# Two attention blocks on one core: full-width matmul passes as two column tiles of 64 in place of four of 32, with constants, one small transfer and the planner's numbers changed

## The chip, the cores and the metric

The kernel runs on one core of a Trainium2 chip. The core has a matrix engine (PE), a vector engine (DVE), a scalar engine (ACT), a general engine (POOL) and a queue engine (SP) that issues transfers; ACT issues some too. Each runs its own stream of instructions in order, and they meet at semaphores. The metric is the device time of one execution in microseconds (us). The median of three runs of the kernel before is 323.95 us (320.75 to 328.06).

## The reference

Two independent blocks, A and B, each on an input of 2,048 rows and 640 columns, with 32 heads of 20 columns. Their outputs stand side by side.

```python
# A: softmax attention
scores = jnp.einsum("bhqd,bhkd->bhqk", q, k) * (Dh ** -0.5)
p = _softmax(scores, axis=-1)
o = jnp.einsum("bhqk,bhkd->bhqd", p, v)
# B: linear attention
phi = lambda t: jnp.where(t > 0, t + 1, jnp.exp(t)) + 1e-6
pq, pk = phi(q), phi(k)
kv = jnp.einsum("bhsd,bhse->bhde", pk, v)
z = jnp.einsum("bhsd->bhd", pk)
num = jnp.einsum("bhqd,bhde->bhqe", pq, kv)
den = jnp.einsum("bhqd,bhd->bhq", pq, z)[..., None] + 1e-6
o = num / den
```

In both, `q`, `k` and `v` are thirds of `x @ wqkv`, and the block ends with `o @ wo`. All inputs are bfloat16.

## The kernel before

**Block A without a score matrix.** The scores are small, so the exponential is taken to second order in them: per head, what a query needs of all keys is a table of sums over products of key columns. For each of 16 row tiles (`t_kv`, L1312) PE makes K and V in two halves of 320 columns; ACT copies and squares; DVE makes the products of key columns (`t_feat`, L1364 and L1369, 1.8 us each, 32 in all); and PE adds the tile into the table (`t_T`, L1390), one 32-column product for each head, 242 columns wide. At the end `t_Tfin` (L1397) turns the table, multiplies it with selection matrices `P` and spreads it with a mask (L1456, into f_Tu). On the query side `t_qj` makes q transposed, SP writes it to DRAM (f_Qd), `t_psi` reads it back shifted into one of three slots (f_big, L1589 and L1590), DVE makes the products of query columns (L1601), and `t_pv` runs twelve passes of 512 columns on f_Tu. `t_norm` sends the sums of the weights through DRAM (f_Rc, f_Nd, f_Rbc) for a reciprocal, and `t_out` multiplies by `wo`. A guard (`t_guard`, and L1625) checks that the scores are in range.

**Block B.** `b_tasks` (L1802) makes K and V, phi of K, and sums `phi(k)` times v over row tiles (`kvmm`, L1839; `kvpost` adds into f_kva). `kvfin` (L1868) masks out what belongs to other heads, and sums phi(k) into f_zn. These 640 numbers are written to DRAM (f_Zd, `z1`, L1891) and read back in another order (`z2`, L1893) to form f_kvZ (`zfin`). The table times `wo` gives f_Md, read back as f_Mp. `qden` then makes phi of q, the denominators (`dmm`, 32 columns wide, L2000), their reciprocals, and `numout` the output.

**Column tiles.** Every matmul pass with up to 128 stationary columns goes through `fm` (L1104). It cuts the stationary operand into pieces of 32 columns, each in its own column strip of the array, and issues a load and a matmul for each. The state products of `t_T`, the small q passes of `t_qs` (L1555), the guard's products, `tmm`, `cmm` and `dmm` place 32-column tiles by themselves and do not go through `fm`. Transposes and the selection products use the full width.

**Order of work.** Nothing of the order is written by hand beyond the loads. Every piece of work is a `_Task` with an engine, an assumed duration, dependencies and a priority. `_Plan.step` (L833) takes the engine and task that can start first by its assumed times, the lower priority number first among those ready together, and emits its instructions. So assumed durations (as in `job`, L1073, where a pass counts columns / 2400 us plus 0.003, or 0.1 if that is more) and the priorities in `_C` (L947) together set the order on every engine. `spd` (L1099) emits transfers to SP or ACT; as the queue is in order, a transfer that waits for a semaphore holds back all behind it.

**Constants.** `consts` makes the identity matrix and clears buffers. `mid_consts` (L1208) makes the rest as one chain of tasks, each after the one before: DVE makes scale vectors (L1225 to L1232), POOL an iota, DVE masks and the memsets of f_kva, f_dn and f_kvN (L1239 to L1249), POOL the selection matrices P (L1257, 17 copies), then five times an iota on POOL into the same buffer and two mask operations on DVE (L1266, L1270, L1271).

Of the kernel before, what the change touches and what calls it, by code (L numbers as in the profile page):

```python
# [6 lines left out]
F32 = mybir.dt.float32  # L7
BF16 = mybir.dt.bfloat16
I32 = mybir.dt.int32
# [921 lines left out]
def _off(d):  # L931

    if d is None:
# [12 lines left out]
_WS = 176  # L946
_C = dict(q=0.62, qs=0.04, ks=0.0, kd=0.02, bk=1.68, bks=0.0, bq=-2.52, bo=0.0, out=2.14, pv=0.0, fe=3.88,  # L947
          psi=5.12, r=-4.73, f=0.5, nm=3.12, op=6.09, kv=1.52, npo=0.16, bqs=0.05, bd=0.02, bn=4.94)


class _Fast:

    AUX = (4, 5, 6, 7)
    GB = 3
    NF = 2
    NK = 3
# [27 lines left out]
    def alloc(self):  # L984
# [36 lines left out]
        self.kvZ = self.sb("f_kvZ", [128, N_DC, 32], BF16)  # L1021
        self.zs = self.sb("f_zs", [128, N_DC, 8], F32)
        self.zn = self.sb("f_zn", [128, 2, N_DC], F32)
        self.M32 = self.sb("f_M32", [128, 32], BF16)
# [25 lines left out]
        self.zt = self.sb("f_zt", [128, 128], BF16)  # L1050
        self.it = rb0[:, 0:360].bitcast(I32).rearrange("p (k n) -> p k n", k=2)
        self.rp = self.sb("f_rp", [128, 4], F32)
# [51 lines left out]
    def fm(self, out, lhsT, rhs, start, stop, reads, writes, inc=True, sgc=False):  # L1104
        m = lhsT.shape[1]
        for j in range(0, m, 32):
            k = min(j + 32, m)
            self.sch.mm(out[j:k], lhsT[:, j:k], rhs, start=start, stop=stop, reads=reads, writes=writes, tp=(0, j),
                        inc=inc and k == m, sgc=sgc)
# [3 lines left out]
    def loads(self):  # L1113
# [44 lines left out]
        def perm(x, c):  # L1158
# [4 lines left out]
        self.ew[0] = plan.add(_Task("none", 0.0, lambda t: None), [plan.add(_Task(  # L1163
            "act", 0.9, lambda x, c=c: perm(x, c), prio=1.0), (e0,)) for c in range(N_DC)])
        self.exB[1] = xpose(self.xB, b2, 1, "xB")
# [5 lines left out]
        def permB(x, c):  # L1171
            self.copy(x.eng, self.wB[:, 0, c, :].rearrange("p (a h) -> p a h", h=N_HEADS),
                      self.w0B[:, c, :].rearrange("p (h a) -> p a h", a=D_HEAD), ("w0B",), (("wB", 0, c),))
        self.ewB[0] = plan.add(_Task("none", 0.0, lambda t: None), [plan.add(_Task(
            "act", 0.75, lambda x, c=c: permB(x, c), prio=2.2), (e1,)) for c in range(N_DC)])
        self.ewoB = plain(self.woB[:], self.Bwo.rearrange("(c p) n -> p c n", p=128), "woB", 0.8)
# [13 lines left out]
    def consts(self):  # L1190
        sch, ps, it = self.sch, self.ps, self.it
        sch.op("dve", lambda e: e.memset(self.zt[:], 0.0), writes=("zt",))
        sch.op("pool", lambda e: e.iota(it[:, 0, 0:128], [[1, 128]], base=0, channel_multiplier=-1), writes=("it0",))
        sch.op("dve", lambda e: e.memset(self.warm[:], 0.0), writes=("warm",))
        sch.op("act", lambda e: e.activation(self.warm[:], self.warm[:], AF.Exp), writes=("warm",))
        sch.op("dve", lambda e: e.tensor_scalar(self.ident[:], it[:, 0, 0:128], 0.0, None, op0=ALU.is_equal),
               reads=("it0",), writes=("ident",))
# [10 lines left out]
    def mid_consts(self):  # L1208
        sch, it, rp, plan = self.sch, self.it, self.rp, self.plan
        scr = self.pqT[:, 0, :].bitcast(F32)  # L1210
        last = self.event(1.5)
        cl = (1.0 + _RNG * _RNG / 8.0) * float(D_HEAD) ** -0.5
        q = 0.5 / D_HEAD

        def task(eng, dur, *ops):
            nonlocal last

            def fn(t):
                for f, r, w in ops:
                    sch.op(eng, f, reads=r, writes=w)  # L1220
            last = plan.add(_Task(eng, dur, fn, prio=2.4), (last,))
        K = ("pqT", 0, 0)

        task("dve", 1.6,
             (lambda e: e.tensor_scalar(rp[:, 0:1], it[:, 0, 0:1], -1.0, None, op0=ALU.mult), ("it0",), ("rp",)),  # L1225
             *[(lambda e, c=c, at=at, v=v: e.tensor_scalar(rp[:, c:c + 1], rp[:, 0:1], at, v, op0=ALU.is_ge, op1=ALU.mult),
# [7 lines left out]

        task("pool", 0.5,
             (lambda e: e.iota(it[:, 1, 0:120], [[1, 6], [6, 20]], base=0, channel_multiplier=-1), (), ("it1",)))
        mf, e6, m32 = scr[0:120, 0:120], scr[0:120, 120:126], scr[:, 128:160]
        task("dve", 1.5,
             (lambda e: e.tensor_scalar(mf, it[0:120, 1, 0:120], 0.0, None, op0=ALU.is_equal), ("it1",), (K,)),  # L1239
             (lambda e: e.tensor_reduce(e6, mf.rearrange("p (h a) -> p h a", a=20), axis=AX.X, op=ALU.add), (K,), (K,)),  # L1240
             (lambda e: e.memset(self.M6[:], 1.0), (), ("M6",)),
             (lambda e: e.tensor_copy(self.M6[0:120, :], e6), (K,), ("M6",)),
             (lambda e: e.memset(self.M1[:], 1.0), (), ("M1",)),
             (lambda e: e.tensor_reduce(m32, self.ident[:].rearrange("p (a h) -> p h a", h=N_HEADS), axis=AX.X,
                                        op=ALU.add), ("ident",), (K,)),
             (lambda e: e.tensor_copy(self.M32[:], m32), (K,), ("M32",)),
             (lambda e: e.memset(self.kvacc[:], 0.0), (), ("kva0",)),
             (lambda e: e.memset(self.mask, 0.0), (), ("mask0",)),
             (lambda e: e.memset(self.kvN[:], 0.0), (), ("kvN0",)))  # L1249
        ops = [(lambda e: e.memset(self.GW[:], 0.0), (), ("GW",)),  # L1250
               (lambda e: e.tensor_copy(self.GW[:, 8:14], self.M6[0:120, :]), ("M6",), ("GW",))]

        for x, (d, r) in enumerate(_SL):
            o = _off(d)[1]
            for a, n, b in ((0, 20 - r, o + r), (20 - r, r, o)):
                if n:
                    ops.append((lambda e, x=x, a=a, n=n, b=b: e.tensor_copy(  # L1257
                        self.P[:, x, 6 * a:6 * (a + n)].rearrange("p (a h) -> p a h", h=6),
                        self.ident[0:123, b:b + n].unsqueeze(2).broadcast_to([123, n, 6])), ("ident",), ("P",)))
        ops.append((lambda e: e.tensor_copy(self.P[:, 0, 120:123], self.ident[0:123, 120:123]), ("ident",), ("P",)))  # L1260
        task("pool", 9.0, *ops)
        m2 = scr[:, 0:168]
        for c in range(N_DC):
            h0, nh = self.hlo[c]
            w = 21 * nh
            task("pool", 0.6, (lambda e, h0=h0, nh=nh, c=c: e.iota(  # L1266
                it[:, 0, 0:21 * nh], [[D_HEAD, nh], [0, 21]], base=D_HEAD * h0 - 128 * c, channel_multiplier=-1), (),
                ("it0",)))
            task("dve", 0.6,
                 (lambda e, w=w: e.tensor_scalar(m2[:, 0:w], it[:, 0, 0:w], 0.0, None, op0=ALU.is_le), ("it0",), (K,)),  # L1270
                 (lambda e, c=c, w=w: e.scalar_tensor_tensor(self.mask[:, c, 0:w], it[:, 0, 0:w], -19.0, m2[:, 0:w],  # L1271
                                                             op0=ALU.is_ge, op1=ALU.mult),
                  ("it0", K, "mask0"), (("mask", c),)))
        return last

# [105 lines left out]
    def t_T(self, t, deps):  # L1381
# [4 lines left out]
        def mms(_):  # L1386
# [7 lines left out]
            yield  # L1394
        return self.job(mms, [240] * N_GRP, deps, prio=0.5, pool=None)

    def t_Tfin(self, last):  # L1397
# [101 lines left out]
        for s in range(self.NS):  # L1499
            def one(_, s=s):  # L1500
                if s == self.NS - 1:
                    sch.barrier(("pool",), ("TTc",) + tuple(("TT", j) for j in range(4)) +
                                tuple(("Tn", k, h) for k in range(2) for h in range(2)))
                sch.barrier(("pool",), keys)
                sch.op("pool", lambda e: e.memset(self.slot[96:128, s, 0, :], 1.0), writes=(("one", s),))
# [296 lines left out]
    def b_tasks(self, start):  # L1802
# [11 lines left out]
        for tc in range(NQC):  # L1814
# [23 lines left out]
            for cs in ((0, 1, 2), (3, 4)):  # L1838
                def kvmm(b, cs=cs):  # L1839
# [9 lines left out]
                    yield  # L1849
                j = self.job(kvmm, [168] * (4 * len(cs)), ks + vs, prio=_C["kv"])  # L1850
                kvprev.append(j)
# [16 lines left out]
        def kvfin(_):  # L1868
# [5 lines left out]
            sch.op("dve", lambda e: e.tensor_reduce(self.zn[:, 0, :], zs, axis=AX.X, op=ALU.add), reads=("zs",),  # L1874
                   writes=("zn0",))
            for c in range(N_DC):
# [11 lines left out]
        def small(e, dst, src):  # L1888
            with self.nc.allow_non_contiguous_dma(reason="640 numbers in all"):
                return e.dma_start(dst, src)  # L1890
        z1 = self.spd([lambda e: small(e, bass.AP(zd.tensor, zd.offset, [[1, 128], [128, N_DC], [1, 1]]), self.zn[:, 0, :])], (kvd,),  # L1891
                      ("zn0",), ("Zd",), prio=0.4, lat=5.0)
        z2 = self.spd([lambda e: small(e, self.zn[:, 1, :], bass.AP(  # L1893
# [8 lines left out]
        def cmm(b):  # L1902
# [6 lines left out]
            yield  # L1909
        cj = self.job(cmm, [24] * 20, (zf,), prio=0.4)  # L1910

# [39 lines left out]
        for c in range(N_DC):  # L1951
            for h in range(2):
# [11 lines left out]
                def mpost(x, j=j, c=c, hc=hc, h=h):  # L1964
# [3 lines left out]
        m1 = self.spd([lambda e: e.dma_start(md.rearrange("(c p) n -> p c n", p=128), self.Mn)], mps,  # L1968
                      tuple(("Mn", c, h) for c in range(N_DC) for h in range(2)), ("Md",), prio=0.4, lat=6.0)
        n = D_MODEL  # L1970
# [9 lines left out]
        def qden(tc):  # L1980
# [19 lines left out]
            def dmm(b):  # L2000
# [4 lines left out]
                yield  # L2005
            j = self.job(dmm, [512] * 5, qs + [zf], prio=_C["bd"])

# [258 lines left out]
```

## Time and profile before

| | |
|---|---|
| median of 3 runs | 323.95 us |
| profiled execution, its own time | 326.26 us |
| span, first to last instruction | 324.1 us |
| PE instructions: matmuls, loads | 6,866 and 6,866 |
| mean granted PE clock | 0.974 |
| bytes moved | 47.6 MB |

Busy time is what an engine spent in instructions, as the profile gives it. PE's matmuls overlap each other, so its busy time is a cover of the time line and not a sum of matmuls. "Issue" is time in which an engine waited for nothing that the profile shows. In stretches of 8 us PE is busy for 6.4 us or more in most, and for under 6 us in those from 40, 72, 152, 192 and 240 us. The times of the three runs lie 2.3% apart.

### The profile page before, as it was taken

The page shows a single profiled execution, that of the slowest core. Times are in us where ns is not written, and L with a number is a line of the kernel's source. Part 1 is how long each engine was busy: PE and PEld are TensorE (multiplying, and loading weights), DVE is VectorE, ACT ScalarE, POOL GpSimd, SP SyncE. Part 2 cuts the span into 40 slices and gives each one's busy share as a digit, 9 for nine tenths or more (in the row PEclk, how much of TensorE's full clock was granted, in tenths as well). Part 3 has the DMA queues.
Part 4 walks back from the last instruction along what each step waited for, and adds up shares of the span by engine and source line. Part 5 has one row for each costly group of instructions (what it writes and reads, how often), then busy time and mean ns, then how long its engine had stood idle before and what let it go on. Part 6 is the DMA issues. An engine that isn't in the chain of part 4 may idle for free.

```text
span 324.1 us, 14979 instructions
## 1 busy us (share of the span) xinstructions
PE 289.9 (89%) x6866; PEld 203.3 (63%) x6866; DVE 249.9 (77%) x341; ACT 190.8 (59%) x390; POOL 10.0 (3%) x35
## 2 busy tenths in 40 slices
PE   6888959997999989998997969997988997999995
PEld 2566725886765645686884857665744453678874
DVE  6699964998959699897698794997978766996310
ACT  3678896987998713343344333547738365536653
POOL 2400000000000100000000000020000000000000
PEclk9799999999999978999799997999999999999999
DMA  8999756841013552736565363477588993534643
GB/s 257 276 198 172 113 88 170 292 110 38 4 34 110 155 161 70 179 72 153 141 175 137 98 174 110 99 201 174 70 215 219 236 203 103 156 120 149 171 169 104
DMA packets 59413, 47.60 MB, mean 147 GB/s; under 512 B 23645, under 2 KB 58265, under 8 KB 59345
## 3 DMA queue, kind: packets, MB, share of 16 engines
q1 hardware_dynamic: 53089, 38.60, 50.3%
q10 hardware_dynamic: 6256, 8.00, 9.2%
q8 instruction: 54, 0.88, 1.2%
q14 instruction: 14, 0.11, 0.2%
HBM read 30.65 MB, written 11.25 MB: 129 GB/s over the span
## 4 chain that ended last, share of the span: by engine, by line
PE 60%; DVE 14%; ACT 11%; DMA 7%; issue 5%; ACTq 1%; SPq 1%; POOL 0%; POOLq 0%; DVEq 0%
PE ps L172 60%; DMA f_Rc<-f_xT 3%; DVE f_big L1369 2%; DVE f_big L1364 2%; ACT f_w L1091 2%; DMA f_Nd<-f_Rc 2%; DMA f_big<-f_Qd 2%; ACT f_big L1091 2%; DVE f_Tu L1456 1%; ACT f_qk L1091 1%; ACT f_wB L1091 1%; ACT f_big L1345 1%; ACT f_Ks L1091 1%; DVE f_big L1601 1%; SPq L1589 1%
## 5 line engine op out<-in xcount | busy, mean ns | idle before, releaser
L1601 DVE TENSOR_TENSOR f_big<-f_big 120x1536 bf16<-120x1536 bf16 (+3 forms) x66 | 67.0, 1016 | 4.2 <-DMA f_big<-f_Qd 2.7
L172 PE MATMUL ps<-f_big,f_Tu 120*32 120x512 bf16 (+4 forms) x968 | 57.4, 373 | 6.0 <-issue 4.5
L172 PE MATMUL ps<-f_wB,f_xB 128*32 128x320 bf16 x1280 | 53.4, 309 | 2.5 <-issue 2.5
L172 PE MATMUL ps<-f_w,f_xT 128*32 128x320 bf16 x1280 | 48.8, 305 | 4.3 <-DVE f_xT L1095 3.0
L172 PEld LDWEIGHTS ps<-f_wB,f_xB 128*32 128x32 bf16 x1280 | 42.5, 100 | 8.8 <-issue 3.3
L172 PEld LDWEIGHTS ps<-f_big,f_Tu 120*32 120x32 bf16 (+2 forms) x968 | 31.5, 97 | 24.8 <-issue 6.2
L172 PEld LDWEIGHTS ps<-f_w,f_xT 128*32 128x32 bf16 x1280 | 34.8, 99 | 15.3 <-DVE f_xT L1095 3.2
L1091 ACT COPY f_xT<-ps 126x512 f32<-126x512 f32 (+3 forms) x33 | 16.8, 530 | 38.1 <-PE ps L172 35.0
L1369 DVE TENSOR_TENSOR f_big<-f_big 128x3200 bf16<-128x3200 bf16 x16 | 29.0, 1820 | 8.2 <-ACT f_big L1091 8.2
L1776 ACT ACTIVATE f_ex<-ps 128x320 f32<-128x320 f32 (+1 forms) x52 | 25.5, 500 | 16.5 <-PE ps L172 13.3
L1091 ACT CAST f_pk<-ps 128x320 bf16<-128x320 f32 (+3 forms) x64 | 25.5, 417 | 15.8 <-PE ps L172 12.7
L1364 DVE TENSOR_TENSOR f_big<-f_big,f_Ks 128x3200 bf16<-128x3200 bf16 x16 | 29.1, 1819 | 0.4 <-ACT f_Ks L1091 0.4
L172 PE MATMUL ps<-f_xT,f_w 128*32 128x512 bf16 (+2 forms) x440 | 27.2, 395 | 1.6 <-ACT f_w L1091 1.0
L172 PE MATMUL ps<-f_wo,f_w 128*32 128x320 bf16 x640 | 26.4, 300 | 0.3 <-ACT f_ex L1776 0.3
L1772 DVE TENSOR_SCALAR f_r<-ps 128x320 f32<-128x320 f32 x32 | 15.2, 486 | 12.5 <-ACT f_ex L1776 10.5
L172 PE MATMUL ps<-f_xB,f_wB 128*32 128x512 bf16 x400 | 23.9, 379 | 0.3 <-ACT f_ex L1776 0.3
L172 PEld LDWEIGHTS ps<-f_wo,f_w 128*32 128x32 bf16 x640 | 18.5, 97 | 5.6 <-ACT f_ex L1776 0.9
L1614 ACT ACTIVATE f_Dq<-f_big 120x512 bf16<-120x512 bf16 (+1 forms) x22 | 13.6, 619 | 13.7 <-DMA f_big<-f_Qd 11.2
L1091 ACT CAST f_qk<-ps 120x512 bf16<-120x512 f32 (+1 forms) x24 | 13.5, 586 | 12.0 <-PE ps L172 11.9
L172 PEld LDWEIGHTS ps<-f_xT,f_w 128*32 128x32 bf16 (+2 forms) x440 | 11.3, 98 | 14.5 <-ACT f_w L1091 2.0
L1091 ACT CAST f_big<-ps 128x320 bf16<-128x320 f32 (+1 forms) x33 | 14.3, 442 | 9.7 <-PE ps L172 9.3
L172 PE MATMUL ps<-f_big,f_Vp 128*32 128x242 bf16 x512 | 16.3, 267 | 3.5 <-DVE f_big L1364 3.1
(126 smaller groups left out, 369.4 us busy)
## 6 DMA issues: line engine op xcount, KB each, us to landing
f_big<-f_Qd SPq DMA_DIRECT2D x20, 480.0 KB, 5.1
f_big<-f_Qd SPq DMA_DIRECT2D x20, 240.0 KB, 6.1
f_Qd<-f_qk SPq DMA_DIRECT2D x20, 120.0 KB, 1.9
f_Rbc<-f_Nd ACTq DMA_DIRECT2D x3, 720.0 KB
f_w<-f_Nd ACTq DMA_DIRECT2D x4, 480.0 KB
out_dram<-f_pk SPq DMA_DIRECT2D x12, 160.0 KB, 3.6
f_wB<-in_B_wqkv_dram SPq DMA_DIRECT2D x2, 800.0 KB, 6.2
out_dram<-f_w SPq DMA_DIRECT2D x8, 160.0 KB, 5.4
```

The source lines that it names most:

```text
L172: lambda e: e.matmul(out, lhsT, rhs, start=start, stop=stop, tile_position=tp, skip_group_check=sgc),
L1091: return self.sch.op("act", lambda e: e.copy(out, in_), reads=reads, writes=writes)
L1345: self.sch.op("act", lambda e: e.activation(F[:, :, 2:22], F[:, :, 222:242], AF.Square), reads=kk, writes=(("F", s, "d"),))
L1364: sch.op("dve", lambda e: e.tensor_tensor(F[:, :, 122:222].rearrange("p h (d a) -> p h d a", a=20), k0.unsqueeze(2).broadcast_to([128, 32, ...
L1369: sch.op("dve", lambda e: e.tensor_tensor(F[:, :, 22:122].rearrange("p h (d a) -> p h d a", a=20), k0.unsqueeze(2).broadcast_to([128, 32, ...
L1456: sch.op("dve", lambda e: e.tensor_tensor(dst.rearrange("p b (v h) -> p b v h", h=nh), src.rearrange("p b (h v) -> p b v h", h=nh), mask.u ...
L1589: fns = [lambda e: e.dma_start(sl[:, 0:4, :], self.q_load(u, 0, 4, 1)), lambda e: e.dma_start(sl[:, 9:11, :], self.q_load(u, 7, 2, 3))]
L1601: sch.op("dve", lambda e: e.tensor_tensor(sl[:, o:o + n, :], sl[:, a:a + 1, :].broadcast_to([120, n, N]), sl[:, b:b + n, :], op=ALU.mult), ...
L1614: sch.op("act", lambda e: e.activation(self.Dq[0:120, dq, 0:N], sl[:, 0, :], AF.Square), reads=(k0,), writes=(("Dq", dq),))
L1772: sch.op("dve", lambda e: e.tensor_scalar(r1, ps[:, j.bank, 0:n], 0.0, 1e-6, op0=ALU.max, op1=ALU.add), reads=(("ps", j.bank),), writes=(( ...
L1776: sch.op("act", lambda e: e.activation(ex, ps[:, j.bank, 0:n], AF.Exp), reads=(("ps", j.bank),), writes=(("ex", k, h),))
```

## The change

`fm` cuts at `TW = 64` columns, so a 128-column pass is two loads and two matmuls; a pass of 120 or 126 columns is one tile of 64 and one of 56 or 62. Direct 32-column products stay as they are.

`mid_consts` becomes tasks with their own dependencies in place of one chain: the iotas get buffers of their own and are made at once on POOL; the memsets of f_kva and f_kvN move from DVE to POOL, after P, with that of f_GW; the memset of the mask (f_dn) becomes a DVE task of its own. The tasks that use these buffers on POOL wait for them by name.

In block B the five columns of f_zn are cast to bfloat16, turned by one full-width matmul with the identity, copied, and written to DRAM as five rows of 128 numbers.

Some assumed durations of the planner change (columns of `t_T`, `kvmm`, `dmm`, `cmm`; ACT's permutes; latencies of two transfers), and most priorities in `_C`.

```diff
-_C = dict(q=0.62, qs=0.04, ks=0.0, kd=0.02, bk=1.68, bks=0.0, bq=-2.52, bo=0.0, out=2.14, pv=0.0, fe=3.88,
-          psi=5.12, r=-4.73, f=0.5, nm=3.12, op=6.09, kv=1.52, npo=0.16, bqs=0.05, bd=0.02, bn=4.94)
+_C = dict(q=0.62, qs=0.04, ks=0.0, kd=-0.005, bk=8.07, bks=0.0, bq=-3.62, bo=0.169, out=1.37, pv=0.0, fe=4.51,
+          psi=7.74, r=-3.6, f=-1.2, nm=0.91, op=4.0, kv=3.3, npo=0.1, bqs=0.0013, bd=0.0, bn=3.56)
...
+    TW = 64
...
     def fm(self, out, lhsT, rhs, start, stop, reads, writes, inc=True, sgc=False):
         m = lhsT.shape[1]
-        for j in range(0, m, 32):
-            k = min(j + 32, m)
+        w = self.TW
+        for j in range(0, m, w):
+            k = min(j + w, m)
...
-            "act", 0.9, lambda x, c=c: perm(x, c), prio=1.0), (e0,)) for c in range(N_DC)])
+            "act", 1.45, lambda x, c=c: perm(x, c), prio=1.5), (e0,)) for c in range(N_DC)])
...
-            "act", 0.75, lambda x, c=c: permB(x, c), prio=2.2), (e1,)) for c in range(N_DC)])
+            "act", 1.3, lambda x, c=c: permB(x, c), prio=2.2), (e1,)) for c in range(N_DC)])
...
+        ti = task("pool", 1.8, (),
+                  (lambda e: e.iota(i1, [[1, 6], [6, 20]], base=0, channel_multiplier=-1), (), ("it1",)),
...
-             (lambda e: e.memset(self.kvacc[:], 0.0), (), ("kva0",)),
-             (lambda e: e.memset(self.mask, 0.0), (), ("mask0",)),
-             (lambda e: e.memset(self.kvN[:], 0.0), (), ("kvN0",)))
...
+        tp = task("pool", 6.0, (ti,), *ops)
+        task("pool", 2.5, (tm, tp),
+             (lambda e: e.memset(self.GW[:], 0.0), (), ("GW",)),
+             (lambda e: e.tensor_copy(self.GW[:, 8:14], self.M6[0:120, :]), ("M6",), ("GW",)),
+             (lambda e: e.memset(self.kvacc[:], 0.0), (), ("kva0",)),
+             (lambda e: e.memset(self.kvN[:], 0.0), (), ("kvN0",)))
...
+        prev = task("dve", 0.42, (tm,), (lambda e: e.memset(self.mask, 0.0), (), ("mask0",)))
...
-        return self.job(mms, [240] * N_GRP, deps, prio=0.5, pool=None)
+        return self.job(mms, [293] * N_GRP, deps, prio=0.5, pool=None)
...
-                sch.barrier(("pool",), keys)
+                sch.barrier(("pool",), keys + ("kvN0", "kva0", "GW", "P"))
...
-                j = self.job(kvmm, [168] * (4 * len(cs)), ks + vs, prio=_C["kv"])
+                j = self.job(kvmm, [290] * (4 * len(cs)), ks + vs, prio=_C["kv"])
...
-        z1 = self.spd([lambda e: small(e, bass.AP(zd.tensor, zd.offset, [[1, 128], [128, N_DC], [1, 1]]), self.zn[:, 0, :])], (kvd,),
-                      ("zn0",), ("Zd",), prio=0.4, lat=5.0)
+        def zmm(b):
+            sch.mm(ps[0:N_DC, b, 0:128], self.zb[:], self.ident[:], start=True, stop=True, reads=("zn0", "ident"),
+                   writes=(("ps", b),))
+            yield
+        zj = self.job(zmm, [128], (kvd,), prio=0.3, mode="full")
+
+        def zpost(x):
+            self.copy(x.eng, self.zr[:], ps[0:N_DC, zj.bank, 0:128], (("ps", zj.bank),), ("zr",))
+        zp = self.any(128, zpost, (zj,), prio=0.3, rel=(("aux", zj),))
+        z1 = self.spd([lambda e: e.dma_start(zd.rearrange("(c p) o -> c (p o)", p=128), self.zr[:])], (zp,),
+                      ("zr",), ("Zd",), prio=0.4, lat=4.0)
...
-        cj = self.job(cmm, [24] * 20, (zf,), prio=0.4)
+        cj = self.job(cmm, [24] * 3, (zf,), prio=0.4)
...
-        j = self.job(dmm, [512] * 5, qs + [zf], prio=_C["bd"])
+        j = self.job(dmm, [590] * 5, qs + [zf], prio=_C["bd"])
```

## The prediction

> **What bounds the kernel now.** I began with the page's busy rows.
>
> ```profile
> PE 289.9 (89%) x6866; PEld 203.3 (63%) x6866; DVE 249.9 (77%) x341; ACT 190.8 (59%) x390; POOL 10.0 (3%) x35
> ...
> q8 instruction: 54, 0.88, 1.2%
> ```
>
> PE is busy for 289.9 us of a 324.1 us span, so only about 34 us of it are idle. The second line, from the DMA queues, says that the instructions themselves come in 54 packets of 16 KB; at 64 bytes each that is 256 to a packet, and 54 x 256 = 13,824 is PE's 6,866 matmuls plus 6,866 weight loads and a few waits. This queue feeds PE.
>
> Is PE's busy time already streaming? The order of time of PE in one stretch of the first half:
>
> ```profile
> 59.74 0.99 PE L172 MATMUL ps<-f_w,f_xT 128*32 128x320 bf16 x24
> 60.56 0.85 PE L172 MATMUL ps<-f_wB,f_xB 128*32 128x320 bf16 x20
> 61.23 1.01 PE L172 MATMUL ps<-f_big,f_Vp 128*32 128x242 bf16 x32
> ```
>
> From 60.56 to 61.23 lie 20 matmuls, five passes of four tiles: 0.67 / 5 = 134 ns a pass of 320 columns. In the starts of single matmuls the four tiles of a pass begin within 10 ns of each other and the passes stand 136 ns apart; passes of 512 columns stand 216 ns apart, of 242 columns 103, of 147 columns 64. All are columns / 2.4 per ns plus 2 to 3 ns. The four tiles run at once, and their weight loads (97 ns each in their rows) are hidden even under a 64 ns pass. So a pass cannot get shorter by having fewer tiles.
>
> Next the chain that ended last, in order of time:
>
> ```profile
> 74.75 2.06 issue
> ...
> 175.59 1.72 issue
> ...
> 192.30 2.36 issue
> ...
> 222.98 2.09 issue
> ...
> 231.98 2.95 SPq L1589
> ...
> 234.98 6.06 DMA f_big<-f_Qd
> ```
>
> And who waited for whom, of PE's weight loads and of SP's queue (us in total, times, longest):
>
> ```profile
> PEld ps L172 <- issue: 16.9, 24, 2.9
> ...
> SPq L1890 <- DMA f_Zd<-f_zn: 11.6, 1, 11.6
> ```
>
> Four stretches of the chain, of about 2 us each, are "issue" on PE: nothing that the profile shows was waited for; the weight loads' longest such wait is 2.9 us. I laid them beside the instruction packets. Packet k mostly starts when PE has issued between 256k + 170 and 256k + 330 instructions. At these four gaps it started at 256k + 430, 413, 449 and 426 (74.05, 174.60, 192.42 and 222.36 us), 4 to 6 us late, and PE came back 2.2 to 2.8 us later. PE had run dry of instructions. Two smaller gaps, 0.39 us at 186.74 and 0.33 at 282.06, have the same signature. Together 2.06 + 1.72 + 2.36 + 2.09 + 0.39 + 0.33 = 8.95 us. After the gap at 192.3 the clock row falls to half for 3.4 us (0.79 over 192 to 200), another 1.7 us.
>
> **The change, part by part.** The sum is made against the profiled execution: span 324.1, its own time 326.26. The median of the runs shown is 323.95, 2.3 lower.
>
> *Two tiles of 64 (the helper `fm`).* 6,120 of the 6,866 matmuls go through `fm`, as four tiles each (rows of f_wB,f_xB 1,280; f_w,f_xT 1,280; f_wo 640; and so on). Half of them go, with half of their loads: 13,732 PE instructions become 7,612. An `fm` pass has four instructions in place of eight.
>
> First, the gaps. Some 240 instructions lie between the early starts, at 256k + 180, and PE running dry, which at full rate is 240 / 8 x 136 ns = 4.1 us, or 6.5 us with 512-column passes. With half the instructions it is 8.2 to 13 us. The latest packet of the 54 started 6.3 us after 256k + 180 and took about 1 us. So I take all six gaps as gone: -8.95, and -1.7 for the clock. Here the Trainium skill speaks the other way: "Runtime: NRT & Kernel Launch", section "Instruction fetch mechanics", has the cost of a block boundary mostly hidden. By it the halving is worth 0; by the rows, 48 of 54 are hidden and six cost 8.95 us. The rows decide. Each of the four lies inside a PE stretch of the chain, but DVE is close behind (7.63 us of 8 busy over 72 to 80), so I pass on 0.8: -8.5. The bounds are 0 (DVE or a transfer is next everywhere) and -10.6.
>
> Second, the switches of width. The state products (L1390), the small q passes (L1555), the range guard's products (L1625), and `dmm`, `cmm` and `tmm` stay at 32 columns. Each now stands between passes of 64. No row shows 64 beside 32. The nearest is 128 beside 32: where a 32-wide pass is followed by a 128-wide transpose without a wait, the start is 229 ns after a 320-column pass (136 is usual), 200 after a 242-column one (103), and 149 after a 128-column transpose on the way back (56): 93 to 97 ns each. The skill's "TensorEngine Tiling (Array Packing)", section "Tiling Modes", says that changing the tiling mode drains the array; this speaks against the change. By the rule every such edge pays; by the trace only an edge to or from 128 is seen to. Stretches of 32: 16 state jobs, 2 small q, 8 guard, 4 `dmm`, 1 `cmm`, 3 `tmm` = 34, so 68 edges x 0.096 = 6.5 us, and 0 if 32 and 64 don't count as a change. I take the row's price for all, and 0.6 of it on the path, as state jobs and guard products often follow a wait: +3.9.
>
> Third, the load in front of a pass that was waited for. Loads last 97 ns with 32 columns and 133 with 120, so about 110 with 64 (my estimate by interpolation): 13 ns at some 30 gaps, +0.4. Under a running pass 110 is less than 136; under the 80 `kvmm` passes of 64 to 71 ns it would cost 80 x 43 = 3.4 us if loads were not pipelined, but loads of 120 columns already run under transposes 56 ns apart, so 0. That two 64-wide tiles stream at once no row shows; the skill's page just named lists 128x64 as two tiles that work independently. I take that, and price the opposite below.
>
> *Constants.* In the order of time before, DVE runs the memsets of f_kva (0.76 us), f_dn (0.41) and f_kvN (0.46) from 7.20 to 8.91, and only then the copy of f_xT for which PE waits (2.99 us, until 9.11). The f_kva and f_kvN memsets go to POOL, the f_dn one becomes a task behind the copies: 1.63 us leave from in front. -1.1 on the path, as K's weight and DVE's later features (8 of 8 us busy at 32 to 40) may take over; between 0 and -1.8. POOL makes six iotas at once (0.25 to 0.29 each) before its 17 copies (5.3 us), all needed only at 112 us or by DVE's masks: nothing, with 100 us of cover. If that cover went, they would cost 1.5 us. DVE's ten mask operations (2.4 us) no longer wait for POOL in turns; counted at 0. The added waits of the three late POOL memsets are for POOL's own earlier work: 0.
>
> *The sums of phi(k).* Now 640 packets of 4 bytes are written (z1, L1891) and SP stands 11.6 us in front of the read-back, from 219.6 to 231.2. Queued behind it are the loads of f_big; the chain runs through them to 241.06, DVE sits 1.7 us, and PE 2.11 until 244.32. The change turns the numbers with one small matmul, copies them (0.3 us) and writes five rows of 512 bytes. The nearest rows, f_Qd<-f_qk, land in 1.9 to 2.9 us, so SP waits some 3 us. The full-width matmul costs two edges, 0.2. I take -2.0; the bounds are +0.5 (SP waits for the copy in place of the landing) and -4.
>
> *Planner's durations and priorities.* They move work without adding any. ACT's five permutes of f_w (7.2 us at 39.4 to 46.5) lie on the chain beside PE gaps of 2.33 and 1.02; what a new order gives or takes elsewhere can't be read from this trace. Value 0, bounds -5 and +8 (PE's other gaps over 0.25 us are some 14 us in all).
>
> Sum: -8.5 + 3.9 + 0.4 - 1.1 - 2.0 = -7.3. Against 326.26 that is 319.0; taken from the median, 323.95 - 7.3 = 316.6. I say 316.5.
>
> **Rivals.**
> - *As summed:* 311 to 320. Chance 0.46.
> - *Edges between 32 and 64 cost nothing, or the new order helps:* -7.3 - 3.9 = -11.2, 313, and with a few us from the order 305 to 311. For: a switch has been seen only to or from full width. 0.18.
> - *The gaps close and the time doesn't follow:* DVE (249.9 busy, full over 56 to 72) or the edges take it back. Then -8.5 falls to about -3 and the sum to -2: 320 to 327. For: DVE is never far behind. Against: the long PE stretches of the chain. 0.21.
> - *It doesn't do what it says:* packets come late by more when PE asks less often, and gaps stay per packet: half of 8.95 remains, 320 to 321. It is inside the case above.
> - *Slower: the 64-wide loads are not hidden, or the two tiles take turns.* The place is every `fm` pass, 6,120 / 4 = 1,530. From 8.5 / 1,530, about 6 ns a pass, the gain is gone, and with 9 the whole change loses. If two loads of 110 had to run one after the other in front of a pass of 320 columns (220 in place of 136) the 986 such passes would add 83 us: 400. At 20 ns a pass it is +31: 347. Against: the hidden loads of 120 columns just named. 0.08.
> - *A worse order:* 328 to 334. 0.07.
>
> About 2% (317.5 and 330.4) is what a measurement of this kernel can tell from no change. From the cases: faster 0.51, same 0.35, slower 0.14. The range, 305 to 328, reaches over the first three cases and leaves out the last two.
>
> **What would show it.** Right: 7,600 PE instructions, about 30 packets of queue q8, no "issue" of 2 us on PE, passes still 136 and 216 ns apart, the first long PE stretch from about 7.5 us, SP's wait for f_Zd at 3 us. Edges of 95 ns would show in the starts around f_Vp's products. Wrong if passes stand further apart than columns / 2.4, or if DVE's waits for PE shrink while PE's waits for DVE and ACT grow by as much as "issue" lost.

## The result, and the profile after

The changed kernel takes 307.39 us (306.53 to 309.48), the kernel before beside it 324.35. The ratio is 0.9522, with a 95% interval of 0.9424 to 0.962: 5% faster. The prediction said 316.5; the range, 305 to 328, holds the result. It lies at the fast end: not in the case held likeliest (311 to 320) but in the second, 305 to 311. Some executions of any of these kernels come out 1.5 to 3% longer, many of them at a lower granted clock; the medians and ratios from here on leave these out. The profiled execution took 307.76 us, with a span of 305.9.

The busy rows and the instruction queue on the page after:

```profile
PE 289.7 (95%) x3807; PEld 194.5 (64%) x3807; DVE 252.3 (82%) x345; ACT 188.1 (61%) x386; POOL 11.5 (4%) x37
...
q8 instruction: 32, 0.52, 0.7%
```

PE is busy for as long as before, 289.7 us against 289.9. What went is its idle time: 306 - 290 = 16 us in place of 34. The instructions come in 32 packets, not 54. The granted clock was 0.981 on the mean, against 0.974: by that, PE ran at half clock for 12 us of the span in place of 17, which is worth 3 us at most (an estimate from these two shares).

The chain in order of time, at its long pieces:

```profile
7.41 3.92 PE ps L172 x30
...
77.27 34.39 PE ps L172 x487
...
233.91 10.35 DMA f_big<-f_Qd
...
247.59 41.60 PE ps L172 x526
```

The first long PE stretch begins at 7.41 us (9.11 before). No "issue" piece of the chain is longer than 0.44 us; the four of 2 us are gone. And the waits of the weight loads, and of DVE for ACT's copies of K:

```profile
PEld ps L172 <- issue: 16.6, 55, 0.9
...
DVE f_big L1377 <- ACT f_big L1094: 3.1, 3, 1.5
```

The longest "issue" wait of a load is 0.9 us (2.9 before). The total is as large, because an edge, the change from one tile width to another, counts here too: 35 of the 55 waits, with 10.2 us of the 16.6, stand at an edge, and none of the 24 before did. In PE's order of time one state product between two `fm` passes is seen with its edge:

```profile
76.83 0.44 PE L172 MATMUL ps<-f_wB,f_xB 128*64 128x320 bf16 x4
77.27 1.01 PE L172 MATMUL ps<-f_big,f_Vp 128*32 128x242 bf16 x32
78.20 2.33 PE L172 MATMUL ps<-f_w,f_xT 128*64 128x320 bf16 x30
```

Eight passes of 242 columns at 103 ns are 0.83 us; the next 64-wide pass starts 0.93 us after the first.

PE's busy time by stage, from the windows of both kernels (us busy of us):

| stage, us of the span | before | after |
|---|---|---|
| 0 to 110 | 97.0 | 104.1 |
| 110 to 140 | 28.0 | 27.6 |
| 140 to 200 | 52.8 | 57.3 |
| 200 to 250 | 45.5 | 49.1 |

The gain is spread: PE is busy for 7 us more in the first stage, and for 4.5 and 3.6 us more in the two from 140 us on. Some of this is edges, which count as busy time.

### The profile page after: what moved, and what is told of

It is laid out like the page before. It is cut to its first block, busy times and chain, and to the rows that moved or that the text cites. A ratio compares the mean times of both kernels' runs of the same rounds, so it can differ in the third digit from the quotient of the medians.

```text
span 305.9 us, 8859 instructions
## 1 busy us (share of the span) xinstructions
PE 289.7 (95%) x3807; PEld 194.5 (64%) x3807; DVE 252.3 (82%) x345; ACT 188.1 (61%) x386; POOL 11.5 (4%) x37
## 4 chain that ended last, share of the span: by engine, by line
PE 71%; DVE 12%; DMA 8%; ACT 5%; issue 1%; ACTq 1%; SPq 0%; POOL 0%; DVEq 0%; POOLq 0%
PE ps L172 71%; DMA f_big<-f_Qd 3%; DVE f_Tu L1464 2%; DMA f_Nd<-f_Rc 2%; DVE f_big L1609 2%; DMA f_w<-f_Nd 2%; DVE f_big L1377 2%; DVE f_big L1372 2%; ACT f_big L1094 1%; ACT f_ex L1784 1%; ACT f_pk L1094 1%; ACT f_Ks L1094 1%; DVE f_r L1780 1%; DVE f_pk L1803 1%; ACTq L1689 1%
## 5 line engine op out<-in xcount | busy, mean ns | idle before, releaser
L172 PE MATMUL ps<-f_big,f_Tu 120*64 120x512 bf16 (+3 forms) x484 | 54.7, 373 | 1.9 <-issue 1.1
L172 PE MATMUL ps<-f_w,f_xT 128*64 128x320 bf16 x640 | 48.7, 307 | 3.1 <-DVE f_xT L1098 2.1
L172 PE MATMUL ps<-f_wB,f_xB 128*64 128x320 bf16 x640 | 47.7, 300 | 1.6 <-ACT f_ex L1784 1.0
L172 PEld LDWEIGHTS ps<-f_w,f_xT 128*64 128x64 bf16 x640 | 35.4, 112 | 14.5 <-DVE f_xT L1098 2.3
L172 PEld LDWEIGHTS ps<-f_big,f_Tu 120*64 120x64 bf16 (+1 forms) x484 | 28.1, 109 | 23.8 <-issue 2.3
L172 PEld LDWEIGHTS ps<-f_wB,f_xB 128*64 128x64 bf16 x640 | 35.8, 110 | 11.0 <-ACT f_ex L1784 1.3
L1094 ACT COPY f_xT<-ps 126x512 f32<-126x512 f32 (+3 forms) x29 | 15.5, 539 | 36.2 <-PE ps L172 33.6
L1094 ACT CAST f_pk<-ps 128x320 bf16<-128x320 f32 (+4 forms) x63 | 25.5, 414 | 10.9 <-PE ps L172 10.6
L172 PE MATMUL ps<-f_xT,f_w 128*64 128x512 bf16 (+3 forms) x240 | 28.2, 404 | 0.0
L172 PE MATMUL ps<-f_wo,f_w 128*64 128x320 bf16 x320 | 23.8, 300 | 0.4 <-DVE f_w L1715 0.3
L172 PE MATMUL ps<-f_xB,f_wB 128*64 128x512 bf16 x200 | 23.7, 379 | 0.1
```

Source lines behind the costliest of these rows:

```text
L172: lambda e: e.matmul(out, lhsT, rhs, start=start, stop=stop, tile_position=tp, skip_group_check=sgc),
L1094: return self.sch.op("act", lambda e: e.copy(out, in_), reads=reads, writes=writes)
```

## The experiments

The theory to start from is the prediction's: half the instructions end the gaps in PE's supply and the edges give part of it back; constants and transfer add a little. This sum left some 9 us unexplained, and the first suspect was what it had counted at 0, the new order of work. The runs were made in three series, each with the kernel before beside it: tiles alone, all but the tiles, the numbers alone and all but the numbers (kernel before 322.1 us); durations, priorities, full width and by stage (326.8); the other four (327.6). Within a series the medians are set beside each other. Across series the kernel before moved by 1.7%, so medians and ratios to it are both given where they differ; a ratio carries about 1% either way, and differences under 3 us are not read.

**The tiles alone.**

```diff
 # the kernel before
+    TW = 64
...
-        for j in range(0, m, 32):
-            k = min(j + 32, m)
+        w = self.TW
+        for j in range(0, m, w):
+            k = min(j + w, m)
```

> The kernel before with two tiles of 64 in its fm helper and nothing else; the planner sees no difference, so every engine's order is that of before. Theory (half the instructions end the four gaps in PE's instruction supply, edges between 32 and 64 columns give some back): 317 to 321 us, no issue gap of over 1 us on PE, some 32 instruction packets in place of 54. Rival A (the tiles are the whole change): 306 to 310. Rival B (the gaps were hidden, the gain lies in the new order): 323 to 328, with PE's waits for DVE and ACT grown by what issue lost.

318.34 us (317.34 to 320.99), ratio 0.9861 (0.9784 to 0.9938): 1.4% or 4.5 us of 324. The prediction's tile terms sum to -8.5 + 3.9 + 0.4 = -4.2.

```profile
PEld ps L172 <- issue: 17.9, 64, 0.5
...
SPq L1892 <- DMA f_Zd<-f_zn: 13.1, 1, 13.1
```

In its trace (granted clock 0.957) no wait of PE for nothing that the profile shows is longer than 0.5 us. Rival A falls, and so does rival B in its strong form. The waits of PE at 42 us (2.31) and of SP for f_Zd (13.1) stayed, as in the kernel before, and PE's wait behind the latter grew from 2.11 to 4.59 us, at 240 us. So a part of what the gaps gave up was lost there again.

**All but the tiles.**

```diff
 # the changed kernel
-    TW = 64
+    TW = 32
```

> The changed kernel with tiles of 32 again; constants, the transfer of the sums and the planner's numbers stay changed. Theory: the constants, the transfer and the new order give the rest of the gain, 4.6 us of it go: 311 to 315, and issue gaps of 2 us are back on PE. Rival A (the tiles are the whole change): 322 to 327. Rival B (all order): 306 to 309.

315.71 us, ratio 0.979 (0.9634 to 0.9946), a little over the theory's 311 to 315. The gaps are back. Its chain in order of time, the issue pieces of over half a us:

```profile
22.12 2.06 issue
...
74.39 1.78 issue
...
147.05 0.86 issue
...
163.42 2.39 issue
...
235.77 3.07 issue
```

They sum to 10.2 us, at other places than before, and each stands where an instruction packet started late: packets 1, 12, 24, 27 and 39 started when PE had issued 256k + 394, 410, 373, 449 and 449. In this order the tiles are worth 315.7 - 307.4 = 8.3 us (8.7 by the ratios), against 4.5 in the old one. PE waits less for other engines here, so more of each gap may be on the path; the two values are not far enough apart to show that.

**The planner's numbers alone.** The durations, the latency of f_Md and `_C` of the change, in the kernel before.

```diff
 # the kernel before
-_C = dict(q=0.62, ... bk=1.68, ... psi=5.12, r=-4.73, f=0.5, ...
+_C = dict(q=0.62, ... bk=8.07, ... psi=7.74, r=-3.6, f=-1.2, ...
...
-        return self.job(mms, [240] * N_GRP, deps, prio=0.5, pool=None)
+        return self.job(mms, [293] * N_GRP, deps, prio=0.5, pool=None)
 # and the durations of perm, permB, kvmm, cmm, dmm
```

> The kernel before with only the planner's assumed durations and the priorities of the change. Theory (the new order, which the prediction counted at 0, made up the 9 us that the sum fell short): 312 to 318, with the PE gaps at 41 to 47 and 152 us gone. Rival (the numbers fit only the new tasks; the order is worth nothing or harms by itself): 322 to 332.

342.09 us, ratio 1.0634 (1.0482 to 1.0787): 6% or 20 us slower. My theory's number was wrong by over 24 us. The chain behind 255 us shows where the time went:

```profile
271.28 10.61 DMA f_Zd<-f_zn
...
281.91 4.95 DMA f_zn<-f_Zd
...
292.38 4.28 DMA f_dc<-f_dn
...
302.89 2.84 DVE f_pq L2028
```

The sums of phi(k) are ready at 271 us; in the kernel before they are at 219, and in the changed one at 199. So the write, the read-back and the denominators, which elsewhere lie beside other work, stand bare near the end: PE stands for 7.63 us until 287 and for 8.38 us until 306. Its granted clock falls to half for 10.2 us at each of the two, which adds to the loss.

**The numbers with the new transfer,** to see whether the slow write made the 342.

```diff
 # the kernel of the numbers alone
-        z1 = self.spd([lambda e: small(e, bass.AP(zd.tensor, zd.offset, [[1, 128], [128, N_DC], [1, 1]]), ...
+        zj = self.job(zmm, [128], (kvd,), prio=0.3, mode="full")
+        zp = self.any(128, zpost, (zj,), prio=0.3, rel=(("aux", zj),))
+        z1 = self.spd([lambda e: e.dma_start(zd.rearrange("(c p) o -> c (p o)", p=128), self.zr[:])], (zp,), ...
```

> The kernel before with the planner's numbers and the new transfer of the sums, old constants, tiles of 32. Theory (without the new constant tasks the planner's greedy order goes another way and block B's K and V end late, whatever the transfer is): 330 to 342, PE gaps of several us after 270 us again. Rival (the slow write of the sums made the 342): 317 to 325.

336.0 us in a single run, 6 us under the 342. Set beside the kernel before of its own series it is 8 us slower, where the numbers alone are 20 us slower, so by this one run the transfer is worth 6 to 12 us here and doesn't undo the harm. Gaps of 6.9, 8.2 and 2.5 us behind 277 us remain, and the sums are ready as late as without it (first line: the numbers alone; second: this kernel):

```profile
L1874 DVE TENSOR_REDUCE f_zn<-f_zs x1: 197/197/197, 271.0 to 271.0; 128x5 f32<-128x40 f32 x1
...
L1876 DVE TENSOR_REDUCE f_zn<-f_zs x1: 197/197/197, 271.2 to 271.2; 128x5 f32<-128x40 f32 x1
```

**The numbers with the new constants,** old transfer and 32-column tiles: `mid_consts` and its buffers as in the change.

```diff
 # the changed kernel
-    TW = 64
+    TW = 32
 # and f_zn written directly, as in the kernel before
```

> The kernel before with the planner's numbers and the new constants, old transfer of the sums, tiles of 32. Theory (numbers and constant tasks belong together): 315 to 321. Rival (the numbers harm without the new transfer): 330 or more.

321.1 us (318.84 and 323.4), ratio 0.9803 (0.9676 to 0.993), at the upper end of the theory's 315 to 321: with the constant tasks the 342 are gone.

```profile
L1882 DVE TENSOR_REDUCE f_zn<-f_zs x1: 196/196/196, 201.8 to 201.8; 128x5 f32<-128x40 f32 x1
```

The sums are ready at 201.8 us, 69 us earlier. The constants are short work (POOL's 17 copies, the longest piece, take 5.3 us), so this is another order: with other tasks the planner assumes other times. Which of the assumed times decides it was not traced, and the constants alone, with the old numbers, were not run. The numbers have no worth of their own: without the constants they cost 20 us.

**All but the numbers.** The changed kernel with durations and `_C` of before.

```diff
 # the changed kernel
-        return self.job(mms, [293] * N_GRP, deps, prio=0.5, pool=None)
+        return self.job(mms, [240] * N_GRP, deps, prio=0.5, pool=None)
 # and _C and the other durations of before
```

> The changed kernel with the durations and priorities of before, so with tiles of 64, the constants and the transfer alone: just the parts that the prediction's sum counted. By that sum: 315 to 319. Rival (the parts were under-counted and the order is nothing): 307 to 311. Rival (the new tasks need new numbers): 322 or more.

317.91 us (316.64 to 318.89), ratio 0.9847 (0.9719 to 0.9975): 1.5% or 5.0 us of 324. The prediction's sum for just these parts was 7.3. That its 316.6 lies so near to 317.9 is in part luck, as the kernel before was at 322.1 in this series and not at 324. Beside the tiles alone, 318.3, the constants and the transfer show no gain in the old order, where the sum had 3.1 us for them.

The numbers on top are worth 317.9 - 307.4 = 10.5 us, by the ratios too. PE's own waits, the idle time in front of its matmuls added up over each trace, tell what the tiles did and what the numbers did (us):

| kernel | PE idle, nothing shown that it waited for | PE idle, waiting for another engine |
|---|---|---|
| before | 9.7 | 20.8 |
| tiles alone | 0.0 | 20.8 |
| all but the tiles | 10.7 | 10.1 |
| all but the numbers | 0.5 | 20.0 |
| changed | 1.1 | 11.2 |

The tiles empty the first column and leave the second; the numbers, with the constants and the transfer, halve the second and leave the first. One place of it is in the waits of DVE for ACT, of the kernel without the numbers:

```profile
DVE f_big L1377 <- ACT f_big L1094: 17.0, 6, 6.3
```

Here ACT runs its ten permuting copies of f_w in one piece, from 38.8 to 46.0 us, and the copies of K stand behind them. In the changed kernel they lie between other work from 41.8 to 80.2 us, and the wait is 3.1.

**Durations alone, priorities alone.** The permutes' own priority (1.0 to 1.5) is in the same line as their duration and goes with the durations.

```diff
 # the changed kernel: one run with the old _C ...
-_C = dict(q=0.62, ... bk=8.07, ...
+_C = dict(q=0.62, ... bk=1.68, ...
 # ... the other with the old durations
-            "act", 1.45, lambda x, c=c: perm(x, c), prio=1.5), (e0,)) for c in range(N_DC)])
+            "act", 0.9, lambda x, c=c: perm(x, c), prio=1.0), (e0,)) for c in range(N_DC)])
```

> The changed kernel with the priorities of before and the new assumed durations. Between it and the one with both old (317.9 us) lie the durations alone. Theory (durations that fit what the work takes let the planner keep PE fed; the priorities refine it): 311 to 315, the PE gaps of over 1 us down from five to two or fewer. Rival (the priorities carry the new order): 316 to 319. Second rival (old priorities fit old durations): over 320.

> The changed kernel with the new priorities and the assumed durations of before. Theory (durations carry it): 314 to 319. Rival (priorities carry it): 307 to 311. Second rival (each set of priorities fits one set of durations, as the 342 us of the numbers without the new tasks hint): over 320, with single PE gaps of 4 us or more.

New durations with old priorities: 315.89 us, ratio 0.963 (0.9569 to 0.9691), a little over the theory's 311 to 315. The wait of DVE for ACT falls to 6.9 us, but gaps of 2.86 us at 146 and 2.65 at 171 come in. New priorities with old durations: 323.55 us, ratio 0.9847 (0.9773 to 0.9921), with a gap of 4.04 us at 244. PE waits for other engines for 20.0 and 22.7 us in these two. Whether each is better or worse than neither is open: by the medians 2 us better and 6 worse, by the ratios 7 us better and the same. But in the same series the kernel with both, at full-width tiles (below), took 306.8: 9 and 17 us less. The second rival of the priorities run holds: a set of priorities fits one set of durations.

**The transfer alone,** taken back out of the changed kernel.

```diff
 # the changed kernel
-        z1 = self.spd([lambda e: e.dma_start(zd.rearrange("(c p) o -> c (p o)", p=128), self.zr[:])], (zp,), ...
+        z1 = self.spd([lambda e: small(e, bass.AP(zd.tensor, zd.offset, [[1, 128], [128, N_DC], [1, 1]]), ...
```

> The changed kernel with the sums written as 640 packets of 4 bytes again: the transfer by itself. By the prediction's sum (2.0 us): 308 to 311, SP waiting over 8 us for the write to land and PE or DVE waiting for loads of f_big behind it. Rival (in the new order nobody needs what is queued behind): 306 to 308.

316.93 us (316.71 to 319.25), ratio 0.9697 (0.9619 to 0.9774): 9.5 us over the changed kernel by the medians, 1.75% or 5.7 us by the ratios. Both are more than the 2.0 that I had given it. Up to 140 us the two kernels agree in every window within 0.1 us of PE's busy time; then, of SP's waits and on the chain:

```profile
SPq L1898 <- DMA f_Zd<-f_zn: 9.5, 1, 9.5
...
212.78 2.33 SPq L1597
...
215.16 9.05 DMA f_big<-f_Qd
```

SP waits 9.5 us for the write to land, the loads of f_big go out after it, and PE stands for 3.17 us at 223 and 1.65 at 260. The planner's order behind the transfer differs too: from 199 us on DVE's instructions come in another order. So the 5.7 to 9.5 us are the wait and the new order together; what each is worth is not separated. PE's waits in all, 18.4 us, are 6 more than in the changed kernel, near the lower of the two values.

**Full-width tiles.**

```diff
 # the changed kernel
-    TW = 64
+    TW = 128
```

> The changed kernel with fm's tile at 128 columns, so one load and one matmul for a pass; same order on every engine. Theory (PE's instruction supply has no gaps left to close at 64, and the edges are as many): 305 to 309; passes stay 136 and 216 ns apart, loads last 98 to 138 ns. Rival (a full-width load is not hidden under the pass before): passes of 180 ns or more for 320 columns, 340 or more in all. Second rival (fewer instructions still pay): 300 to 304.

306.81 us (305.96 to 308.03), ratio 0.9352 (0.9279 to 0.9424). By the medians it is the same as at 64, by the ratios 1.7% less; no gain is shown. Passes stay at 136 and 216 ns, the 80 passes of 147 to 168 columns at 64 to 72. The instructions come in 20 packets. One group of its loads:

```profile
L172 PEld LDWEIGHTS ps<-f_wB,f_xB 128*128 128x128 bf16 x320 | 30.5, 98 | 15.8 <-ACT f_ex L1784 1.3 <-ACT f_pk L1094 0.9 <-issue 0.7
```

A load of 128 columns in one piece lasts 98 ns, less than one of 64 (110) or of 126 (136). The loads stay hidden, and at 64 PE's supply had only 1.1 us of gaps left to close.

**32 columns while state products remain, 64 after.**

```diff
 # the changed kernel
-        w = self.TW
+        w = self.TW if getattr(self, "tp_last", None) is not None and self.tp_last.end is not None else 32
```

> The changed kernel with fm's tile at 32 while state products remain to be issued and at 64 after; same order on every engine. It takes the 32 edges around the state products away (32 x 0.1 = 3.2 us of PE) and brings eight instructions a pass back for the first 110 us. Theory (edges cost about 0.1 us each on PE, and the gaps follow the density of instructions): PE's busy time 3 us lower, one or two issue gaps of some 2 us in the first 110 us and none behind; 306 to 310. Rival (edges are hidden by waits): 309 to 312, PE busy unchanged. Second rival (the gaps have nothing to do with the density): no gap, 303 to 306.

309.1 us (307.83 to 310.16), 2.3 us over full width in the same series. The chain has two issue pieces of over half a us, both in the part with eight instructions a pass:

```profile
63.16 1.83 issue
...
73.23 2.33 issue
```

Their packets started at 256k + 429 and 430. The gaps follow the density of PE's instructions. By the starts of the passes, what they are late at edges adds up to 3.2 us in place of 7.2, a fall of 4.0 where 3.2 was expected. PE's busy time falls by only 1.4, to 288.3 us, where the theory had 3, and the two gaps add 4.2 us. So what fewer edges are worth in time is not shown.

**A try at a faster kernel:** full-width tiles, and the planner told of the widths.

```diff
 # the changed kernel with TW = 128
-    def job(self, mms, cols, deps, prio=3.0, mode="pv", pool="aux", due=None):
+    def job(self, mms, cols, deps, prio=3.0, mode="full", pool="aux", due=None):
...
-        return self.job(mms, [293] * N_GRP, deps, prio=0.5, pool=None)
+        return self.job(mms, [240] * N_GRP, deps, prio=0.5, pool=None, mode="pv")
 # and mode="pv" for the other 32-wide jobs
```

> The changed kernel with full-width tiles in fm, and the planner told which jobs are 32 wide, so that it prefers to keep them together, with the edge priced once and the durations of those jobs without it. A try at a faster kernel. Theory (fewer edges, PE still fed): 303 to 307. Rival (any new order is a new draw, and the priorities fit the old one): 308 to 320.

320.13 us (319.14 to 321.36), 13 us over full width without this (4.6% by the ratios). Its waits have one line that was not there:

```profile
PE ps L172 <- DVE f_w L1715: 11.2, 1, 11.2
```

PE stands for 11.2 us at 270, waiting for DVE's product that block A's output is made of. The rival's 308 to 320 is met at its edge, and its reason, that priorities fitted to one model are a new draw with another, fits the two runs of durations and priorities. With new priorities it may be faster; that was not tried.

## Why the prediction was right, and where it fell short

*The gaps.* Right. All six are gone with half the instructions, come back with the old tiles (10.2 us), and come back in just the stage to which 32-column tiles are given back. The mark of a gap is less sharp than the prediction had it. The four large gaps before, the five of the second order and the two of the stage run had their packet start at 256k + 373 to 449. The two small gaps had 356 and 350, and packets at 359 and 349, and one at 380 in the second order, stood before no gap at all. The half clock behind the gap at 192 us is gone too; the prediction had passed over a second such stretch, 3.4 us behind a wait of 2.12 us for ACT at 155, which went with the new order and not with the tiles.

*The edges.* Right in size: in the trace a 64-wide pass starts 206 ns after a 242-column one (103 is usual), and a state product 232 ns after a 320-column pass (136 is usual): 103 and 96 ns, as taken from full width beside 32. With the tiles alone what passes are late at edges adds up to 7.2 us, against 1.4 in the kernel before: 5.8 more, where the prediction had 6.5. The sum of the tile terms, -4.2, met the -4.5 of the tiles alone. But the interval of that run reaches from -2.0 to -7.0, and the two shares in the sum, 0.8 of the gaps and 0.6 of the edges on the path, were measured by nothing; so the agreement speaks for the sum and not for each of them.

*Two tiles at once, and their loads.* Right: passes at 136 and 216 ns, loads at 110 ns. The slower rival, loads not hidden, did not happen even at 64 ns passes.

*Constants.* The first long stretch begins 1.7 us earlier (1.63 expected). What of it reached the end was not measured alone: constants and transfer together, -3.1 in the sum, came to -0.4 in the old order, as PE's waits grew elsewhere. That the constants also set the planner's order was not in the sum: without them the same numbers made 342 and 336 us.

*The sums of phi(k).* SP's wait of 11.6 us is gone, and of the 3 us that were expected to stay nothing did: the write goes out at 204.3 us, and when SP comes to the read-back at 209.2 it has landed. I gave it -2.0 with -4 as the bound, from the gap beside it in the old order. In the new order it is worth 5.7 to 9.5 us, the changed order behind it included. So this term was mis-sized for the order in which it came to stand. That a stopped queue costs more where PE has less slack is one reading of it; the runs don't separate it from the order.

*Planner's durations and priorities.* The step that failed. "Value 0, bounds -5 and +8" treated the new order as if it were any order. The measured effect is -10.5 on top of the other parts, outside the bounds on one side, and +20 without the new constants and the transfer, outside on the other. What it acts on is PE's waits for other engines, 20.0 us without it and 11.2 with it. The trace did show one place to which it applied: five permutes that the planner took for 0.9 us each and that lasted 1.4, in front of PE gaps of 2.33 and 1.02 us. I named it and gave it nothing. Both gaps are gone. The other places were not traced one by one.

Added in this order, the tiles gave 4.5 us, the constants and the transfer about 0.5, and the planner's numbers 10.5, which makes the 15.5 of the ratio. So the tile terms met their run, the small terms did not show in the old order, and the forecast was short by what the new order gave. That the result is inside the range is owed to the width of the range: it took in the second case, which asked for free edges or a helpful order. The edges were not free; the order helped, by more than that case had for it.

## What to carry to other kernels

Lay the instruction packets beside an engine's unexplained gaps. If they start late by the count of instructions issued, try fewer and larger instructions; here that paid until the gaps were gone, and going on from 64 to 128 columns showed no more. When an order comes from a greedy planner, its assumed times, its priorities and the list of tasks are one thing, to be measured together; a part of it taken alone can be worth less than nothing. And price a transfer that holds an in-order queue by what is queued behind it in the new order; here the old order gave 2.0 us and the new one 5.7 to 9.5.

## What the runs showed of the hardware

In the full-width run a weight load of 128 columns lasts 98 ns, one of 126 columns 136, one of 120 between 133 and 150, and one of 32 takes 96; in the changed kernel one of 64 takes 110. So time grows with columns, except that exactly 128 is short.

A change between 64- and 32-column tiles makes the next pass start 96 to 103 ns late, about as much as one between 128 and 32 (93 to 97 before the change, 93 ns in the full-width run at a state product after a 320-column pass). A matmul with a single stationary column followed a 32-wide pass of 320 columns as any other pass would before (136 ns), but 233 ns after a 64-wide one: it behaves like a 32-wide tile.

Where PE stood for 7.63, 8.38 and 11.2 us (the numbers alone, and the try at a faster kernel), the granted clock was at half for 10.2 us from some point of the wait on. Of the gaps of about 2 us in the kernel before, those that ended at 154.7 and 194.7 us were followed by 3.4 us at half, and those that ended at 76.8, 177.3 and 225.1 were not.
